# V of batch 1 through SyncE's hardware queue: a blockwise causal attention with a maxout MLP on one core

## The chip, the core and the metric

One core of one Trainium2 chip runs the whole program. The metric is the device time of one execution in microseconds, the median of several executions; smaller is better.

## What is computed

```python
B, H, S, D = 8, 8, 576, 64                       # attention: 8 batches, 8 heads
scores = q @ k.T / sqrt(D)                       # causal by blocks of 64: block_i >= block_j
attn   = softmax(scores)
x      = (attn @ v).transpose(0, 2, 1, 3).reshape(B * S, H * D)      # 4608 x 512
out    = maximum(x @ w1, x @ w2) @ w_out         # 512 -> 1024 -> 512, float32
```

The inputs q, k, v and the weights are float32 in HBM; the matmuls run in bf16.

## The kernel before

**Tiling.** Heads are worked in pairs: pair p is two heads of batch p // 4, and a group g is two pairs, so group g holds pairs 2g and 2g+1. There are 32 pairs, 16 groups and 8 batches. For each group, q and k come as fp32 (`load_qk`, one DMA each on SyncE's queue, L120), are cast to bf16 (`cast`, L132, nearly always on GpSimd), transposed by TensorE (L352) and copied out of PSUM (L360) to `qT` and `kT`. Scores (L371, L389) go through ACT's exp (L395) to `aT`, GpSimd zeroes the masked corners (`mask`, L400), and `av` (L479) multiplies by V. DVE divides by the row sums (L485, L486) and writes `xp`. `x_out` brings `xp` transposed into `xT`: TensorE transposes (L517, L519), and two copies (L522, L523), on DVE unless other engines are given. From group 4 on, DMA transposes do it instead (L497).

**xT** is one tile of 128 partitions, 4 rows (`NDM`) of 4672 bf16 columns each; a row holds 128 of the 512 model features, and columns are tokens. `x_out` of group g = 2b + u writes rows 2u and 2u+1 in one copy, at the tokens of batch b. Late tokens of `xT` are not needed early, so parts of them hold other data at first: `w2_sb`, the four blocks of w2, lies in row 1 (three blocks of 1024 columns from token 1536 on) and row 3 (one block).

**The MLP.** max(a, b) = b + max(a - b, 0), so the kernel forms d = w1 - w2 (`diff_w`, DVE, L162), h = x d, g = max(h, 0) (L220, DVE), and out = x M + g w_out with M = w2 w_out (`bT_unit` L227 and L229, `m_unit` L238 and L243). These matmuls are cut into units that generators yield one by one; `fill(n)` places the next ones between the steps of attention, and units become ready when the tokens they need are in `xT`.

**Order.** The schedule is manual: each engine runs its instructions in the order in which the program issues them. The framework adds the semaphore waits, from which parts of which tiles an instruction reads and writes. `load_qk(..., gated=True)` first issues a one-column memset on GpSimd into the tile to be loaded, so that the DMA on SyncE can start only when GpSimd has got to that point.

**V.** `load_v(b, c)` loads rows c of batch b by GpSimd's software queue (L136), which casts to bf16 on the way, into `vv_r[b % 3]`, a buffer of 5 chunks x 8 heads x 65 columns (the 65th holds ones, for the row sums). Chunks 0 to 3 have 128 rows, chunk 4 has 64. For batch 1 the five loads are issued in the opening part, between the loads of group 3 and an `x_out`:

```python
    load_qk(3, (SP, SP), gated=True)    # L651
    for c in range(NCH):
        load_v(1, c)                    # L653
    x_out(0, 2, NCH)                    # L654: rows 0, 1 of xT, tokens 256 to 575
    diff_w(1)
    fill(2)
```

A little later come `x_out(1, 2, NCH)` (L663: rows 2 and 3, the same tokens), the casts of group 3, and `pool_work(4)`, which issues the gates and loads of group 4 (L544). Batch 1 is first used by `av` of pair 4.

Of the kernel before, what the change touches and what calls it, by code (L numbers as in the profile page):

```python
# [8 lines left out]
FP32 = mybir.dt.float32  # L9
# [5 lines left out]
def kernel(  # L15
# [10 lines left out]
    nc = tc.nc  # L26

    B, H, S, D = q.shape
    P = 128
    BLK = 64  # L30
# [23 lines left out]
    NCH = 5  # L54
# [39 lines left out]
    NV, NA, NT = 3, 4, 4  # L94
# [3 lines left out]
    vv_r = [ring.tile([P, NCH, H, D + 1], BF16, name=f"vv{r}") for r in range(NV)]  # L98
    aT_r = [ring.tile([P, 2, AW + APAD], BF16, name=f"aT{r}") for r in range(NA)]
    xT = ring.tile([P, NDM, NTOK + BLK], BF16, name="xT")  # L100
# [9 lines left out]
    dve, pool, act = nc.vector.tensor_copy, nc.gpsimd.tensor_copy, nc.scalar.copy  # L110

    def load_qk(g, queues, gated=False):
        b, u = divmod(g, GPB)
        for nm, src, queue in (("q", q, queues[0]), ("k", k, queues[1])):
            if queue is None:
                continue
            raws[nm, g] = t = raw.tile([P, 2, RPP * D], FP32, name=f"{nm}raw")
            if gated:
                nc.gpsimd.memset(t[:, 0, :1], 0.0)
            queue.dma_start(  # L120
                out=t[:],
                in_=src[b, 4 * u:4 * u + 4].rearrange(
                    "(s h) (p t) d -> (h p) s (t d)", h=2, t=RPP),
            )

    def cast(nm, g, parts):
        t = raws[nm, g].rearrange("p s (t d) -> p t s d", d=D)
        if (nm, g) not in qk_n:
            qk_n[nm, g] = qkn.tile([P, RPP, 2, D], BF16, name=f"{nm}n")
        n = qk_n[nm, g]  # L130
        for copy, j0, j1 in parts:
            copy(out=n[:, j0:j1], in_=t[:, j0:j1])  # L132

    def load_v(b, c):
        rows = min(P, S - c * P)
        nc.gpsimd.dma_start(  # L136
            out=vv_r[b % NV][P - rows:, c, :, :D],
            in_=v[b, :, c * P:c * P + rows, :].rearrange("h p d -> p h d"),
        )

    w1r = moe_w1.rearrange("(c p) f -> p c f", p=P)
    w2r = moe_w2.rearrange("(c p) f -> p c f", p=P)
# [4 lines left out]
    for j in range(d_ff // WB):  # L147
        row, n = (1, j) if j < 3 else (3, 0)
        t0 = 3 * S - 3 * BLK + n * NDM * WB
# [21 lines left out]
    dve, pool, act = nc.vector.tensor_copy, nc.gpsimd.tensor_copy, nc.scalar.copy  # L171
# [19 lines left out]
    for c in range(2):  # L191
        load_v(0, c)
# [310 lines left out]
    def x_out(g, t0=0, t1=NCH, copies=(dve, dve)):  # L503
        b, u = divmod(g, GPB)
        if x_by_dma(g):
            if u == GPB - 1:
                done_tokens[0] = (b + 1) * S
            return
        xp = xps[g]
        n = t1 - t0  # L510
        n_odd = min(t1, NCH - 1) - t0
        pe = ps_m.tile([P, 2, n, BLK], BF16, name="ps_xe", tag="m")
        po = ps_m.tile([P, 2, n_odd, BLK], BF16, name="ps_xo", tag="m")
        for s in range(2):
            for t in range(t0, t1):
                src = xp[:, s, t].rearrange("p a d -> p (a d)")
                nc.tensor.transpose(pe[:, s, t - t0, :], src[:BLK], ident[:BLK, :BLK])  # L517
                if t < NCH - 1:
                    nc.tensor.transpose(po[:, s, t - t0, :], src[BLK:], ident[BLK:, BLK:])  # L519
        dst = xT[:, 2 * u:2 * u + 2, b * S + t0 * P:b * S + t1 * P].rearrange(  # L520
            "p s (t h w) -> p s t h w", h=2, w=BLK)
        copies[0](out=dst[:, :, :, 0], in_=pe[:])  # L522
        copies[1](out=dst[:, :, :n_odd, 1], in_=po[:])  # L523
        if u == GPB - 1:
            done_tokens[0] = min(b * S + t1 * P, (b + 1) * S)
# [8 lines left out]
    def fill_of(g):  # L534
        if g == NG - 1:
            return 45
        left = 5 - g if g < 5 else 2 - (g - 5) % 2
        return -(-max(0, ready() - KEEP) // left)


    def pool_work(s):
        g, i = divmod(s, 2)
        if s == 4:
            load_qk(4, (SP, SP), gated=True)  # L544
        elif s == 5:
            load_qk(5, (SP, SP), gated=True)
            cast("q", 4, ((pool, 0, RPP),))
            cast("k", 4, ((pool, 0, RPP),))
        else:
            if i == 1 and g + 3 < NG:  # L550
                load_qk(g + 3, (SP, SP), gated=True)
            if i == 1 and g + 2 < NG:
                cast("q", g + 2, ((pool, 0, RPP),))
                cast("k", g + 2, ((pool, 0, RPP),))
            nb, j = divmod(s + 2, HP)
            if nb < B:
                for c in ((0, 1), (2, 3), (4,), ())[j]:
                    load_v(nb, c)
# [33 lines left out]
    for c in range(2, NCH):  # L592
        load_v(0, c)
# [56 lines left out]
    pad_keys(5)  # L650
    load_qk(3, (SP, SP), gated=True)  # L651
    for c in range(NCH):
        load_v(1, c)  # L653
    x_out(0, 2, NCH)  # L654
    diff_w(1)
    fill(2)
# [14 lines left out]
    n = fill_of(GPB)  # L671
    fill(n // 2)
    transposes("q", 3, (dve, act))()
    pool_work(4)
    fill(n // 3)
    transposes("k", 3, (dve, act))()
    pad_keys(6)
    pad_keys(7)
    pool_work(5)
    fill(n - n // 2 - n // 3)  # L680

    for g in range(GPB + 1, NG):
        a, b = 2 * g, 2 * g + 1
        old = done_tokens[0]
        if x_due:
            x_out(x_due.pop())
        n, new = fill_of(g), done_tokens[0]
        region(tile_0(a), tile_1(a))
        lo, hi = max(3, n // 18), n * 2 // 9
        for p, tiles in ((a, lambda: (tile_2(a), tile_0(b))), (b, lambda: (tile_1(b), tile_2(b)))):  # L690
            if p == a and x_by_dma(g - 2):
                done_tokens[0] = old
            rest = fill(hi)
            done_tokens[0] = new
            fill(rest)
            av_with(p - LAG, lo)
            if p % 2 and x_by_dma(g - 1):
                x_dma(g - 1)
            copy_out = t_pair(p)
            outs = tiles()  # L700
            copy_out()
            region(*outs)
            if p % 2 and g + 1 < NG:
                pad_keys(p + 1)
                pad_keys(p + 2)
            pool_work(p)
        x_due.append(g - 1)
        fill(n - 2 * (lo + hi))
# [49 lines left out]
```

The softmax here doesn't subtract the row's maximum and nothing guards it: scores larger than these inputs give would overflow.

## Time and profile before

| | |
|---|---|
| median of 3 runs | 258.6 us (258.4 to 258.81) |
| the profiled execution: its own time | 260.0 us |
| span of the profiled execution, first to last instruction | 258.2 us |
| granted TensorE clock over the span | 1.00 |
| PE busy | 247.4 us (96%) |
| DVE / ACT / POOL busy | 136.1 / 143.2 / 110.4 us |
| HBM read / written | 34.60 / 9.44 MB |
| V loads on GpSimd's queue | 40 (32 of 128 KB, 8 of 64 KB by their bf16 size), 33.7 us of issue on POOL |

How to read it: times in the views are microseconds from the start of the span, unless marked ns. PE is TensorE's matmuls, PEld its weight loads, DVE VectorE, ACT ScalarE, POOL GpSimd, SP SyncE; an engine with a q behind it is its sequencer. A line such as L522 is a line of the kernel before. In a timeline a row gives start, length, engine, line, operation, tiles (out<-in), shape, count, and in brackets the idle time before it with what ended it. In the chain of waits a row gives start, length, and what the end of the program was waiting for then. In a table by stretches, each engine's busy time stands with its number of instructions, followed by the granted clock, the mean share of the 16 DMA engines (over 1 where packets of one engine overlap) and GB/s.

### The profile page before, as it was taken

How to read it: one execution, taken by the hardware profiler on the slowest of the kernel's cores; microseconds unless marked ns; L12 is line 12 of the kernel's file. 1: busy time of each engine (PE TensorE's matmuls, PEld its weight loads, DVE VectorE, ACT ScalarE, POOL GpSimd, SP SyncE). 2: the span in 40 equal slices, each digit the busy share in tenths (PEclk: the TensorE clock that was granted, in tenths of full speed). 3: DMA queues.
4: the chain of work that ended last, by engine and by line, in shares of the span. 5: the costliest groups of instructions: out<-in, count | busy, mean ns of one | idle time of the engine just before them, and what ended most of it. 6: DMA issues, size and time to landing. Idle time of an engine off the chain costs nothing.

```text
span 258.2 us, 7195 instructions
## 1 busy us (share of the span) xinstructions
PE 247.4 (96%) x2983; PEld 139.1 (54%) x2983; DVE 136.1 (53%) x299; ACT 143.2 (55%) x200; POOL 110.4 (43%) x274
## 2 busy tenths in 40 slices
PE   7598899799999999999999999999999999999995
PEld 2346678646555555555555554546464655444444
DVE  4967986556584428451845184518550853443200
ACT  2798854476574857586757665766576431000111
POOL 1987950584637263726382638163813010000000
PEclk9999999999999999999999999999999999999999
DMA  6999999499569995998599949985977122202122
GB/s 244 316 206 307 217 251 246 156 102 253 129 162 257 144 188 135 245 154 225 114 244 143 186 145 224 168 196 141 91 109 110 44 56 80 83 0 81 43 104 99
DMA packets 71265, 41.30 MB, mean 160 GB/s; under 512 B 53568, under 2 KB 58048, under 8 KB 71232
## 3 DMA queue, kind: packets, MB, share of 16 engines
q1 hardware_dynamic: 28544, 31.27, 43.4%
q0 software_dynamic: 42272, 8.92, 39.9%
q10 hardware_dynamic: 416, 0.66, 0.7%
q8 instruction: 23, 0.38, 0.6%
q14 instruction: 10, 0.08, 0.1%
HBM read 34.60 MB, written 9.44 MB: 171 GB/s over the span
## 4 chain that ended last, share of the span: by engine, by line
PE 84%; DMA 8%; POOL 3%; ACT 2%; issue 1%; DVE 0%; SPq 0%; POOLq 0%; ACTq 0%
PE ps_y L257 36%; PE ps_h L215 22%; PE ps_o L479 10%; PE ps_s L371 8%; DMA qraw<-in_q_dram 5%; DMA kraw<-in_k_dram 3%; PE ps_qT L352 2%; PE ps_kT L352 2%; PE ps_w L341 1%; ACT aT L395 1%; PE ps_y L272 1%; PE ps_M L238 1%; POOL kn L132 1%; PE ps_s L389 1%; ACT qT L360 1%
## 5 line engine op out<-in xcount | busy, mean ns | idle before, releaser
L395 ACT ACTIVATE aT<-ps_s 128x1024 bf16<-128x1024 f32 (+2 forms) x100 | 95.8, 996 | 25.8 <-PE ps_s L371 24.2
L257 PE MATMUL ps_y<-wo_sb,g 128*128 128x512 bf16 x280 | 69.8, 379 | 0.0
L215 PE MATMUL ps_h<-xT,d_sb 128*128 128x512 bf16 (+3 forms) x320 | 69.2, 358 | 0.3 <-DVE d_sb L162 0.3
L220 DVE TENSOR_SCALAR g<-ps_h 128x512 bf16<-128x512 f32 (+3 forms) x80 | 50.7, 636 | 30.6 <-PE ps_h L215 28.8
L400 POOL MEMSET aT<- 64x128 bf16 x124 | 22.4, 200 | 81.8 <-ACT aT L395 81.2
L485 DVE RECIPROCAL rec<-ps_o 128x4 f32<-128x4 f32 (+1 forms) x64 | 12.1, 188 | 62.5 <-PE ps_o L479 61.7
L215 PEld LDWEIGHTS <-d_sb 128*128 128x128 bf16 x320 | 29.0, 98 | 29.1 <-issue 2.7
L479 PEld LDWEIGHTS <-aT 128*128 128x128 bf16 x960 | 37.2, 98 | 13.5 <-issue 0.8
L262 ACT COPY y<-ps_y 128x512 f32<-128x512 f32 x31 | 18.2, 587 | 44.5 <-PE ps_y L257 36.1
L257 PEld LDWEIGHTS <-g 128*128 128x128 bf16 x280 | 25.8, 98 | 29.8 <-issue 2.0
L479 PE MATMUL ps_o<-vv,aT 128*128 128x65 bf16 x960 | 39.8, 194 | 0.0
L257 PE MATMUL ps_y<-m_sb,xT 128*128 128x512 bf16 x140 | 38.2, 380 | 0.0
L136 POOL DMA_DIRECT2D vv<-in_v_dram x40 | 33.7, 848 | 1.6 <-issue 1.2
L371 PE MATMUL ps_s<-qT,kT 64*128 64x64 bf16 (+6 forms) x344 | 31.2, 280 | 1.6 <-ACT kT L360 0.7
L486 DVE TENSOR_TENSOR xp<-ps_o,rec 128x256 bf16<-128x256 f32 (+1 forms) x64 | 31.4, 491 | 2.2
L360 ACT COPY qT<-ps_qT 128x576 bf16<-128x576 bf16 (+1 forms) x17 | 10.3, 614 | 19.9 <-PE ps_qT L352 19.9
L132 POOL CAST qn<-qraw 128x1152 bf16<-128x1152 f32 (+1 forms) x16 | 16.9, 1058 | 9.1 <-DMA qraw<-in_q_dram 9.1
L257 PEld LDWEIGHTS <-xT 128*128 128x128 bf16 x140 | 12.2, 98 | 15.1 <-issue 3.5
L371 PEld LDWEIGHTS <-kT 64*128 64x128 bf16 x344 | 12.3, 94 | 11.0 <-issue 6.2
L132 POOL CAST kn<-kraw 128x1152 bf16<-128x1152 f32 (+1 forms) x15 | 17.1, 1140 | 1.4 <-DMA kraw<-in_k_dram 1.4
L360 ACT COPY kT<-ps_kT 128x576 bf16<-128x576 bf16 x15 | 9.6, 639 | 14.4 <-PE ps_kT L352 14.4
L207 POOL COPY g<-g 128x512 bf16<-128x512 bf16 x8 | 4.9, 614 | 20.7 <-DVE g L220 20.3
(58 smaller groups left out, 161.8 us busy)
## 6 DMA issues: line engine op xcount, KB each, us to landing
qraw<-in_q_dram SPq DMA_DIRECT2D x16, 576.0 KB, 5.0
out_dram<-y SPq DMA_DIRECT2D x35, 256.0 KB, 3.7
kraw<-in_k_dram SPq DMA_DIRECT2D x15, 576.0 KB, 5.8
vv<-in_v_dram POOLq DMA_DIRECT2D x32, 128.0 KB, 5.7
w1raw<-in_moe_w_dram POOLq DMA_DIRECT2D x4, 512.0 KB, 8.1
xT<-in_moe_w_dram POOLq DMA_DIRECT2D x4, 256.0 KB, 8.6
wo_sb<-in_moe_w_out_dram POOLq DMA_DIRECT2D x2, 512.0 KB, 10.0
kraw<-in_k_dram ACTq DMA_DIRECT2D x1, 576.0 KB, 5.6
```

The costliest lines, as they stand in the source:

```text
L132: copy(out=n[:, j0:j1], in_=t[:, j0:j1])
L136: nc.gpsimd.dma_start(out=vv_r[b % NV][P - rows:, c, :, :D], in_=v[b, :, c * P:c * P + rows, :].rearrange("h p d -> p h d"),)
L215: nc.tensor.matmul(pt[:, :w], d_sb[:, c, f * P:(f + 1) * P], xT[:, c, t0:t0 + w], start=(c == 0), stop=(c == NDM - 1),)
L220: nc.vector.tensor_scalar_max(g[:, f, m:m + w], pt[:, :w], 0.0)
L257: nc.tensor.matmul(py[:], lhs, rhs, start=(n == 0), stop=(n == len(terms) - 1),)
L262: (dve if i < 2 else act)(out=y[:], in_=py[:])
L360: (copy or copies[i])(out=t[:, p0 * RPP:p1 * RPP].rearrange("q (p j) -> q p j", j=RPP), in_=pts[i][:, :, p0:p1].rearrange("q j p -> q p j"),)
L371: nc.tensor.matmul(ps[:, hh, col:col + w], kT[r, k0:k0 + P], qT[r, q0:q0 + w], start=True, stop=True,)
L395: nc.scalar.activation(out=aT_r[p % NA][:, :, a0:a0 + w], in_=ps[:, :, :w], func=AF.Exp, scale=scale,)
L400: (eng or nc.gpsimd).memset(aT_r[p % NA][BLK:, :, a0:a0 + BLK], 0.0)
L479: nc.tensor.matmul(po[:, gi, hh, :], a[:, hh, a0:a0 + P], vv[:, c, h0 + 2 * hh, :], start=(mm == 0), stop=(mm == n_mm - 1),)
L486: nc.vector.tensor_mul(xp[:, :, ts[0]:ts[0] + n, p % 2].rearrange("q s t d -> q t s d"), po[:, :, :, :D], rec[:, :n].to_broadcast([P, n, 2 ...
```

## The change

V of batch 1 no longer goes by GpSimd's queue. `stage_v` puts it, still fp32, by SyncE's hardware queue into parts of `xT` that no token needs yet: chunks 0 to 2 in row 0 (three slots of 1024 bf16 columns from token 1536 on), chunks 3 and 4 in row 2 (two slots). The five transfers stand where the five `load_v` stood, so on SyncE's queue they come after q and k of group 3 and before those of group 4. In `pool_work(4)`, behind the gates of group 4, GpSimd casts the five chunks into `vv_r[1]`. All other batches are as before.

```diff
+    def v_stage(c):
+        row, n = (0, c) if c < 3 else (2, c - 3)
+        t0 = 3 * S - 3 * BLK + n * 2 * H * D
+        return xT[:, row, t0:t0 + 2 * H * D].bitcast(FP32).rearrange("p (h d) -> p h d", h=H)
+
+    def stage_v(b, c):
+        rows = min(P, S - c * P)
+        nc.sync.dma_start(
+            out=v_stage(c)[P - rows:],
+            in_=v[b, :, c * P:c * P + rows, :].rearrange("h p d -> p h d"),
+        )
+
+    def cast_v(b, c, copy):
+        rows = min(P, S - c * P)
+        copy(out=vv_r[b % NV][P - rows:, c, :, :D], in_=v_stage(c)[P - rows:])
...
         if s == 4:
             load_qk(4, (SP, SP), gated=True)
+            for c in range(NCH):
+                cast_v(1, c, pool)
...
     load_qk(3, (SP, SP), gated=True)
     for c in range(NCH):
-        load_v(1, c)
+        stage_v(1, c)
     x_out(0, 2, NCH)
```

## The prediction

> **What bounds the kernel now.** I first read the busy times: PE is busy for 247.4 of 258.2 us, so idle PE time is 10.8 us in all, and only that can be won. Then the chain of waits, from 24 to 48 us, the part that the change touches:
>
> ```profile
> 26.58 1.14 POOL kz L378 x2
> ...
> 28.34 8.94 DMA kraw<-in_k_dram
> 37.27 0.05 issue
> 37.33 1.15 POOL kn L132
> ...
> 38.55 7.51 DMA qraw<-in_q_dram
> ...
> 46.18 1.16 POOL qn L132
> 47.34 0.05 issue
> 47.38 0.44 PE ps_qT L352 x18
> ```
>
> The chain runs over k of group 3, its cast, the gate, q of group 4 and its cast; PE then waits for that cast. From 48 us on the chain is PE alone. PE's timeline shows the two places that matter:
>
> ```profile
> 27.51 1.04 PE L215 MATMUL ps_h<-xT,d_sb 128*128 128x256 bf16 x8
> ...
> 47.38 0.44 PE L352 MATMUL ps_qT<-ident,qn 64*128 64x64 bf16 x18 [1.61 <-POOL qn L132]
> ```
>
> The second row has the only large gap after 28 us, 1.61 us: all that faster loads here can win. Before the first row stands DVE, which from 25 to 34 us works with hardly a break:
>
> ```profile
> 24.98 0.75 DVE L360 COPY kT<-ps_kT 128x576 bf16<-128x576 bf16 x1
> 25.64 0.35 DVE L522 COPY xT<-ps_xe 128x384 bf16<-128x384 bf16 x1
> 25.91 0.28 DVE L523 COPY xT<-ps_xo 128x256 bf16<-128x256 bf16 x1
> 26.11 1.22 DVE L162 TENSOR_TENSOR d_sb<-w1raw,xT 128x1024 bf16<-128x1024 f32 x1
> ```
>
> The copies at 25.64 are `x_out(0, 2, NCH)`, issued just behind the V loads. PE's h at 27.51 needs the `d_sb` that ends at 27.33. Last, the table by stretches, for the DMAs (last columns: clock, DMA share, GB/s):
>
> ```profile
> 27.30:31.40 4.10, 3.75 (x64) 3.13 (x61) 4.07 (x10) 3.69 (x6) 4.10 (x9) 1.00 1.44 195
> 31.40:36.40 5.00, 4.59 (x51) 3.31 (x48) 4.20 (x9) 4.03 (x5) 2.99 (x10) 1.00 1.26 302
> 36.40:39.50 3.10, 3.10 (x40) 2.23 (x39) 2.82 (x6) 0.64 (x1) 1.23 (x3) 1.00 2.34 157
> 39.50:42.50 3.00, 3.00 (x45) 2.23 (x43) 2.05 (x5) 0.64 (x1) 0.60 (x4) 1.00 2.01 173
> ```
>
> By the packet records, q and k of group 3, issued at 27.8 and 28.3, get their first packet at 31.5: until then the weight loads on GpSimd's queue hold the engines, and they end at 37.3. The last q, k packets go at 36.0 on most engines, 36.85 on the slowest; k lands at 37.28. V of batch 1 runs mainly from 35 to 41.5.
>
> **What the Trainium skill says.** "DMA: Bandwidth & Descriptors", section "Queues, rings and completion order": each DMA engine takes descriptors of one ring in order and alternates between rings. The trace agrees as far as it goes (SP's load of group 3 shares the engines with the weights from 31.5 on); so V on SP's ring comes after q and k of group 3. Section "SWDGE vs HWDGE vs iDMA": only GpSimd's queue casts in flight, which is why fp32 is staged and five casts are added; no run here shows it. Section "Why small descriptors are slow": a 256-byte packet takes 11 cycles of a DMA engine, 3 of them overhead. The trace's 256-byte packets on SP's queue (DMA transposes) take 18 ns, against 93 ns for 2304 bytes, so they are dearer per byte. "TensorE: Matmul & The Clock Gate", Part 1: an idle window of about 3.4 us halves the clock, and a busy one restores it. The trace shows the recovery: the first warm-up matmuls start every 0.43 us, and from 4.1 us on every 0.22.
>
> **The change part by part.**
>
> *Removed from POOL*: five DMA issues, 27.73 to 31.92, 4.19 us. They lie beside POOL's wait for exps (the masks that follow come when ACT lets them), so they bring nothing by themselves.
>
> *Added to POOL*: five casts of 128x512. The cast of 128x1152 takes 1.06 to 1.14 us, so a cast takes some 0.5 us by size and five 2.6 us. They stand between the gate of group 4 and `pad_keys`, where POOL waits 3.13 us for kT (41.69 in the trace of before), and hide there if V has landed by then: 0. With the cover gone they would delay `pad_keys`, the gates of group 5 and the cast of q of group 4, which PE takes at 47.38, by up to 2.6 us.
>
> *Added to SP*: five DMAs of 1024 (the last 512) packets of 256 bytes, behind q, k of group 3, ahead of those of group 4. The issue of q takes 0.37 us and of a transpose, with 640 packets, about 1.3; even at 2 us each the first three are out by 35, before the engines have finished k. SP has nothing else before 38.5. Group 4 then follows V in the ring.
>
> *A new wait on DVE, which the diff doesn't show.* In the compiled order with its waits, the xT copy of `x_out(0, 2, NCH)`, which waited only for PE, now waits also for the landings of V chunks 0, 1 and 2; that of `x_out(1, 2, NCH)` waits for chunks 3 and 4. The data don't overlap: tokens 256 to 575 are written, V lies from 1536 on. But the copy covers two rows, and taken as one run of addresses from row 0, token 256 to row 1, token 575 it holds all of row 0 behind token 256: chunks 0 to 2. Rows 2 and 3 likewise hold chunks 3 and 4. The w2 blocks in rows 1 and 3 are in neither run, and there before has no such wait. So the framework must be taking runs, not elements.
>
> *Its cost.* DVE reaches the copy at 25.64, when V isn't even issued. V's packets start when k of group 3 is through: 36.0 to 36.85, less a little as V no longer competes on the other ring; I take 36.4. Chunks 0 to 2 are 3072 packets, 192 for each of 16 engines. The price of such a packet from HBM isn't in the trace. From below: on GpSimd's queue V's packets (256 bytes read, 128 written) pass at 1205 in one us, or 13.3 ns per engine: 2.55 us. From above: twice the 18 ns of the transposes' packets, 6.9 us. I take 18 ns, 3.46 us. The end adds 0.4 (k: last packet 36.85, landing 37.28). Landing: 36.4 + 3.5 + 0.4 = 40.3 (39.3 to 43.7). DVE is late by 40.3 - 25.64 = **14.7 us** (13.7 to 18.1).
>
> *Who waits.* Behind the copy on DVE stand `d_sb`, the copies of bT, the divisions, g. PE does bT, two tiles of scores and one `av`, and stops at the h of 27.51, whose PSUM buffer and `d_sb` both want DVE. ACT and the masks run dry, POOL stops at the masks of pairs 4 and 5, and the gate of group 4 waits there. The end moves by the whole 14.7. The second copy (30.33 before, 4.7 after the first) finds chunks 3 and 4 landed, as they need 96 more packets, 1.7 us: 0.
>
> *Given back*: q, k of group 3 and V wait in SBUF when work resumes; the casts follow the masks at once, the gate of group 4 comes about 1.6 us earlier against PE's work (masks to 34.55, two casts of 1.15, so 36.9 where it was 38.5), and its loads find idle DMA engines (5.0 us is the median landing). The gap of 1.61 us goes: -1.6 (bounds -1.6 and 0).
>
> *Clock*: after 15 us of idleness PE starts slow. Over some 3 us it would lose 1.5, of which the DVE-bound stretch absorbs part: +1.0 (0.3 to 1.5).
>
> *Sum*: +14.7 - 1.6 + 1.0 = +14.1 us. On the profiled execution that is a span of 258.2 + 14.1 = 272.3 and a time of 260.0 + 14.1 = 274.1; the median of before lies 1.4 below its profiled execution, and so 258.6 + 14.1 = **272.7 us**.
>
> **Rivals.**
> 1. *V's packets cost twice* (36 ns): the landing at 43.7, +18.1 - 1.6 + 1.5 = +18: 276.6. For it: small packets are dear per byte. Against it: 18 ns on the same queue. 0.12.
> 2. *V lands early*: the hardware ring gets its turn sooner with V in it. V can't be issued before 28.8; with the 3.5 us of the fastest V landing in the trace, and three chunks, hardly before 33: +7.4 - 1.6 + 1.0 = +6.8: 265.4. Against it: q of group 3 got nothing before 31.5. 0.08.
> 3. *It does what it seems to*: the wait costs nothing, V stays off the second ring, q of group 4 lands before PE wants it, and the 1.61 us go: 257.0. For it: the 173 GB/s of 39.5 to 42.5, where both rings compete. It decides if chunks 0 to 2 land before DVE arrives at 25.64, which the gate at 27.7 excludes, or if that wait isn't there. 0.02.
> 4. *Nothing*: what is won and a short wait cancel: 258.6. 0.01.
>
> **How the numbers follow.** The likeliest case has 0.77 and gives 272.7; its own bounds are 271.0 (13.3 ns: 13.7 - 1.6 + 0.3 = +12.4) and 274.4 (27 ns, half-way to rival 1: 5.2 us of packets, +16.4 - 1.6 + 1.0 = +15.8). The range takes in rival 1 with a margin, and at the lower end goes beyond 271.0 towards rival 2, since k of group 3 may finish sooner with no V on the other ring: 268.5 to 277.5. A measurement of this kernel tells apart about 0.2%, 0.5 us. Faster by more: 0.02; within: 0.01; slower: 0.97, all cases but the last two.
>
> **What would show it.** In the profile of the changed kernel: a gap of about 15 us on DVE ahead of the xT copy, ended by a DMA into xT; one on PE ahead of h (before: 27.51), then slow matmuls for some 3 us; no gap ahead of qT of group 4; the chain through V's DMA; POOL casts of 0.5 us with no wait. An xT copy still at 25.6, or V landing before 33, would make it wrong.

## The result and the profile after

| | before | after |
|---|---|---|
| median of 4 runs | 258.58 us | 275.5 us |
| lowest to highest | 258.4 to 258.81 | 274.59 to 277.28 |
| profiled execution: time, span | 260.0, 258.2 us | 275.6, 273.8 us |
| mean granted TensorE clock | 1.00 | 0.969 |

The ratio is 1.0662 (95% interval 1.0608 to 1.0716): the changed kernel is 16.9 us slower. The prediction was slower by 14.1, at 272.7, in a range of 268.5 to 277.5.

In the changed kernel's file the lines from `load_w` to `pool_work` stand 16 higher (the xT copy is L538, h L231, av L495, qT and kT L368). Its chain of waits (start, length, what) now runs through the staging of V:

```profile
29.00 0.64 SPq L148
...
29.68 11.08 DMA xT<-in_v_dram
...
40.88 0.09 DVE xT L538
...
41.16 0.28 DVE xT L539
41.44 1.14 DVE d_sb L178
...
42.63 1.89 PE ps_h L231 x8
```

The entry at 29.68 is the third V chunk, from its issue on SP to its landing at 40.76. DVE's timeline shows who waited for it (in brackets the idle time before the row, and what ended it):

```profile
24.95 0.75 DVE L376 COPY kT<-ps_kT 128x576 bf16<-128x576 bf16 x1
40.88 0.36 DVE L538 COPY xT<-ps_xe 128x384 bf16<-128x384 bf16 x1 [15.18 <-DMA xT<-in_v_dram]
41.16 0.28 DVE L539 COPY xT<-ps_xo 128x256 bf16<-128x256 bf16 x1
41.35 1.22 DVE L178 TENSOR_TENSOR d_sb<-w1raw,xT 128x1024 bf16<-128x1024 f32 x1
```

Before, the same copy started at 25.64 with no gap: it is 15.24 us late. On PE's timeline the gap stands ahead of h, as the prediction placed it, and there is none ahead of qT of group 4 (62.80):

```profile
26.73 0.92 PE L495 MATMUL ps_o<-vv,aT 128*128 128x65 bf16 x24
42.63 1.89 PE L231 MATMUL ps_h<-xT,d_sb 128*128 128x256 bf16 x8 [14.98 <-DVE d_sb L178]
...
57.49 0.44 PE L368 MATMUL ps_kT<-ident,kn 64*128 64x64 bf16 x18
...
62.80 0.43 PE L368 MATMUL ps_qT<-ident,qn 64*128 64x64 bf16 x18
```

The eight h matmuls take 1.89 us, where they took 1.04. The table by stretches tells why: the column behind POOL's is the granted clock, and it is 0.50 for the first 5.8 us after the gap:

```profile
27.30:42.50 15.20, 0.34 (x12) 0.22 (x8) 1.62 (x4) 1.34 (x2) 0.40 (x2) 0.64 1.11 225
42.50:48.30 5.80, 5.67 (x44) 3.95 (x45) 5.24 (x11) 2.85 (x4) 0.34 (x2) 0.50 0.00 0
48.30:60.00 11.70, 11.58 (x139) 8.42 (x137) 8.41 (x17) 5.19 (x8) 7.04 (x18) 0.99 0.31 103
```

On GpSimd the five casts run without a wait, 0.62 us each where 0.5 was predicted, and q of group 4 is cast well before PE takes it:

```profile
54.11 2.97 POOL L155 CAST vv<-xT 128x512 bf16<-128x512 f32 x5
...
59.40 1.14 POOL L132 CAST qn<-qraw 128x1152 bf16<-128x1152 f32 x1
```

### The profile page after: what moved, and what is told of

Its sections match the earlier page's. It is cut to its first block, busy times and chain, and to the rows that moved or that the text cites. A ratio compares the mean times of both kernels' runs of the same rounds, so it can differ in the third digit from the quotient of the medians.

```text
span 273.8 us, 7176 instructions
## 1 busy us (share of the span) xinstructions
PE 246.6 (90%) x2949; PEld 140.6 (51%) x2983; DVE 136.4 (50%) x299; ACT 143.3 (52%) x200; POOL 108.2 (40%) x274
## 4 chain that ended last, share of the span: by engine, by line
PE 84%; DMA 6%; ACT 4%; issue 2%; DVE 2%; SPq 0%; ACTq 0%; DVEq 0%
PE ps_y L273 33%; PE ps_h L231 23%; PE ps_o L495 10%; PE ps_s L387 8%; DMA xT<-in_v_dram 4%; ACT aT L411 3%; PE ps_M L254 3%; PE ps_qT L368 2%; DMA qraw<-in_q_dram 2%; PE ps_kT L368 2%; PE ps_y L288 1%; DVE qn L132 1%; PE ps_w L357 1%; PE ps_bT L243 1%; PE ps_s L405 1%
## 5 line engine op out<-in xcount | busy, mean ns | idle before, releaser
L231 PE MATMUL ps_h<-xT,d_sb 128*128 128x512 bf16 (+3 forms) x306 | 69.2, 364 | 16.5 <-DVE d_sb L178 15.0
L273 PE MATMUL ps_y<-wo_sb,g 128*128 128x512 bf16 x275 | 69.1, 379 | 0.4 <-issue 0.3
L231 PEld LDWEIGHTS <-d_sb 128*128 128x128 bf16 x320 | 29.7, 100 | 44.9 <-DVE d_sb L178 15.1
L495 PEld LDWEIGHTS <-aT 128*128 128x128 bf16 x960 | 37.2, 98 | 13.5 <-issue 0.8
L495 PE MATMUL ps_o<-vv,aT 128*128 128x65 bf16 x960 | 39.8, 194 | 0.0
L273 PE MATMUL ps_y<-m_sb,xT 128*128 128x512 bf16 x128 | 36.5, 380 | 1.2 <-issue 0.8
L387 PE MATMUL ps_s<-qT,kT 64*128 64x64 bf16 (+6 forms) x344 | 31.5, 283 | 1.9 <-ACT kT L376 0.7
L136 POOL DMA_DIRECT2D vv<-in_v_dram x35 | 29.4, 845 | 1.6 <-issue 1.2
L132 POOL CAST qn<-qraw 128x1152 bf16<-128x1152 f32 (+1 forms) x16 | 16.9, 1057 | 4.6 <-DMA qraw<-in_q_dram 4.6
L376 DVE COPY kT<-ps_kT 128x576 bf16<-128x576 bf16 (+2 forms) x19 | 12.9, 686 | 0.5 <-PE ps_kT L368 0.5
```

Source lines behind the costliest of these rows:

```text
L136: nc.gpsimd.dma_start(out=vv_r[b % NV][P - rows:, c, :, :D], in_=v[b, :, c * P:c * P + rows, :].rearrange("h p d -> p h d"),)
L231: nc.tensor.matmul(pt[:, :w], d_sb[:, c, f * P:(f + 1) * P], xT[:, c, t0:t0 + w], start=(c == 0), stop=(c == NDM - 1),)
L273: nc.tensor.matmul(py[:], lhs, rhs, start=(n == 0), stop=(n == len(terms) - 1),)
L376: (copy or copies[i])(out=t[:, p0 * RPP:p1 * RPP].rearrange("q (p j) -> q p j", j=RPP), in_=pts[i][:, :, p0:p1].rearrange("q j p -> q p j"),)
L387: nc.tensor.matmul(ps[:, hh, col:col + w], kT[r, k0:k0 + P], qT[r, q0:q0 + w], start=True, stop=True,)
L495: nc.tensor.matmul(po[:, gi, hh, :], a[:, hh, a0:a0 + P], vv[:, c, h0 + 2 * hh, :], start=(mm == 0), stop=(mm == n_mm - 1),)
```

## The experiments

The theory: the xT copy waits for V's landings because the framework takes a copy over two rows of xT as one run of addresses; that wait is nearly the whole loss, and the half clock after it the rest. The main rival: the staging itself is dear (fp32, 256-byte packets, issues on SP, casts). All comparisons are with the kernel before run beside them on the same chip; its median there was 258.99, 258.74 and 259.06 us in the three groups e1 to e4, e5 to e8, e9 and e10. The changed kernel was not run again beside them: its 275.5 us belong to the 258.58 of the table above.

### Is it the wait? e1, e2 and e10

**e1** moves only the place of the staging.

```diff
-    for c in range(NCH):
-        stage_v(1, c)
     x_out(0, 2, NCH)
+    for c in range(3):
+        stage_v(1, c)
...
     x_out(1, 2, NCH)
+    for c in range(3, NCH):
+        stage_v(1, c)
```

> The changed kernel with only the place of the staging altered: chunks 0 to 2 are issued behind x_out(0, 2, NCH), chunks 3 and 4 behind x_out(1, 2, NCH). Same queue, same slots, same casts. Theory (the wait of the xT copy for the landings is the whole loss): DVE's gap of 15.2 us is gone, the xT copy stands near 25.6 again; q and k of group 3 have SP's ring for themselves until V follows, q of group 4 lands near 44 instead of 46, so that PE's gap of 1.61 us ahead of qT of group 4 goes too: 257.0 us, between 256.6 and 258.6. Rival (fp32 V with 256-byte packets and its back-pressure on SP is itself dear): SP is held until 39.5 by V's issues, q of group 4 lands after 47, av of pair 4 waits for the casts: 260 us or more.

259.54 us, ratio to before 1.0017 (1.0002 to 1.0031): above what the theory gave, below the rival's 260. DVE's timeline has the copy back in its place, with no gap:

```profile
25.38 0.75 DVE L376 COPY kT<-ps_kT 128x576 bf16<-128x576 bf16 x1
26.04 0.35 DVE L538 COPY xT<-ps_xe 128x384 bf16<-128x384 bf16 x1
```

**e2** leaves the staging where it is and splits the copies by row.

```diff
+        if g < 2 and t0:
+            for s in range(2):
+                copies[0](out=dst[:, s, :, 0], in_=pe[:, s])
+                copies[1](out=dst[:, s, :n_odd, 1], in_=po[:, s])
+        else:
             copies[0](out=dst[:, :, :, 0], in_=pe[:])
             copies[1](out=dst[:, :, :n_odd, 1], in_=po[:])
```

> The changed kernel with the staging where it is, but the xT copies of x_out for groups 0 and 1 (second part) split into one copy for each row of xT. Theory (the framework takes a copy over two rows as one run of addresses): a copy of one row holds no staged chunk, the wait is gone although V is issued ahead of it; the four extra copies, about 0.2 us each, lie in the stretch where DVE bounds PE: 257.0 + 0.5 = 257.5 us, between 257 and 259. Rival (the wait comes from the order of the program, any writer of xT behind the staging waits): 275.5 us as the changed kernel.

259.50 us, ratio 1.0017 (0.9998 to 1.0036), again a little above what was expected. Its DVE timeline (L540 and L541 are the copies of one row):

```profile
24.99 0.75 DVE L376 COPY kT<-ps_kT 128x576 bf16<-128x576 bf16 x1
25.66 0.25 DVE L540 COPY xT<-ps_xe 128x192 bf16<-128x192 bf16 x1
25.82 0.21 DVE L541 COPY xT<-ps_xo 128x128 bf16<-128x128 bf16 x1
```

The same elements of the same tile are written behind the same staging, and the wait is gone: what decides is not the order of the program but the span of one access. The four copies end at 26.3 where two ended at 26.2, so the split costs about 0.1 us, not 0.5.

**e10** adds the wait to the kernel before: V goes by GpSimd's queue as it did, and chunks 0 to 2 are also staged, where nothing reads them (`stage_v` as in the change).

```diff
     for c in range(NCH):
         load_v(1, c)
+    for c in range(3):
+        stage_v(1, c)
     x_out(0, 2, NCH)
```

> The kernel before, V of batch 1 by GpSimd's queue as it was, and in addition chunks 0 to 2 staged in xT by SP ahead of x_out(0, 2, NCH), where nothing reads them. Only the wait of the xT copy and its transfers are added; no cast, no chunk left out on GpSimd. Theory (the wait for those landings is the loss): the two streams of V share the engines from 36 us on, so the landing is 1 to 4 us later than the 40.8 us of the changed kernel: 276 to 280 us. Rival (the loss needs what else changed: casts on GpSimd, V missing from its queue): under 262 us.

280.03 us, ratio 1.0810 (1.0782 to 1.0838), at the upper end of what was expected, with the copy 4.9 us later than in the changed kernel:

```profile
45.79 0.36 DVE L538 COPY xT<-ps_xe 128x384 bf16<-128x384 bf16 x1 [19.80 <-DMA xT<-in_v_dram]
```

So the wait, with the transfers that it waits for, makes the loss without the rest of the change, and without the wait the rest of the change costs about 0.5 us. That e1 and e2 did not reach the 257.0 and 257.5 that were expected is taken up with e5.

### How long the wait is: e3

Only chunk 0 is staged ahead of the copy; 1 and 2 follow it, 3 and 4 stand as in e1.

```diff
-    for c in range(NCH):
-        stage_v(1, c)
+    stage_v(1, 0)
     x_out(0, 2, NCH)
+    for c in (1, 2):
+        stage_v(1, c)
```

> The changed kernel with only chunk 0 issued ahead of x_out(0, 2, NCH); chunks 1 to 4 behind the x_outs as in e1. Theory (DVE waits for the last landing in the run of addresses that it writes): chunk 0 was issued at 28.36 and took 10.3 us, so DVE resumes near 38.7 instead of 40.9 and the end comes some 2.1 us sooner than in the changed kernel: 273.4 us. Rival (what costs is q and k of group 3 in the ring ahead of V, whatever the number of chunks, or the cold clock alone): the same to within 0.5 us as the changed kernel, 275 to 276.

273.21 us, ratio 1.0579 (1.0538 to 1.0620); DVE's row:

```profile
39.20 0.36 DVE L538 COPY xT<-ps_xe 128x384 bf16<-128x384 bf16 x1 [13.26 <-DMA xT<-in_v_dram]
```

The gap is 1.92 us shorter for two chunks less. In the changed kernel chunk 1 landed at 39.7 and chunk 2 at 40.76: about 1.05 us for each chunk of 1024 packets. So of 15 us two come from the number of chunks. The rest is that V is issued 2.7 us after DVE is ready for the copy (28.36 and 25.70) and then stands behind q and k of group 3, the last of which lands at 36.8; that order itself was not varied.

### The clock: e4

The changed kernel with matmuls of zeros in PE's gap, into a PSUM buffer that nobody reads:

```diff
     av(3, [2, 3, 4])
+    pw = ps_s.tile([P, 2, 512], FP32, name="ps_keep", tag="s")
+    for _ in range(64):
+        nc.tensor.matmul(pw[:, 0], zeros[:, :P], zeros[:], start=True, stop=True)
```

> The changed kernel with 64 matmuls of zeros into a free PSUM buffer behind av of pair 3, which keep PE busy for some 13.8 us of its 15 us gap; nothing reads them. Theory (the half clock after the gap costs the 1.85 us by which PE's work is later at kT of group 3 than DVE was at its copy): no stretch at half clock, 275.5 - 1.9 = 273.6 us, and a spread from run to run as small as before (0.2 us instead of 2.7). Rival (DVE bounds that stretch, and the clock costs next to nothing): 275.0 to 276 us.

273.99 us, ratio 1.0586 (1.0558 to 1.0613), 1.5 below the changed kernel. The granted clock is 1.00 throughout, and PE's timeline has the eight h matmuls at 1.05 us again:

```profile
28.35 13.97 PE L679 MATMUL ps_keep<-zeros 128*128 128x512 bf16 x62
43.16 1.05 PE L231 MATMUL ps_h<-xT,d_sb 128*128 128x256 bf16 x8 [0.84 <-DVE d_sb L178]
```

The wait is still there: the xT copy starts at 41.42, after a gap of 15.15 us. From that copy to PE's kT of group 3 pass 14.63 us here (to 56.05) and 16.61 in the changed kernel (40.88 to 57.49). Before it was 14.76, from 25.64 to this row:

```profile
40.40 0.44 PE L352 MATMUL ps_kT<-ident,kn 64*128 64x64 bf16 x18
```

The half clock costs 2.0 us by the traces and 1.5 by the medians. The four runs went from 273.59 to 274.18, those of the changed kernel from 274.59 to 277.28; that the half clock makes that spread is not shown, since the executions of 275.6 and 277.28 have the same mean clock, 0.969.

### What the median of before contains: e5, e6, e7

The kernel before twice more and e1 once more, one profiled execution each, no edit.

> The kernel before, unchanged, for a second profile. Theory (the 1.4 us by which the profiled execution of before lay above its median are the 1.61 us gap ahead of qT of group 4, which other executions don't have or have shorter): an execution near 258.5 us shows a gap ahead of qT of group 4 of at most 0.5 us, with the loads of group 4 landing before 45. Rival (the gap is in every execution and the 1.4 us lie elsewhere, in the opening or at the end): a gap of 1.3 to 1.9 us whatever the time.

> The kernel before, unchanged, for a third profile. As for e5: by the theory the time moves with the gap ahead of qT of group 4, about one for one; by the rival the gap stays at 1.3 to 1.9 us and the time doesn't follow it.

> The kernel of e1 unchanged, for a second profile. Its median was 259.54 us where its profiled execution ran 259.37 with a gap of 0.16 us ahead of qT of group 4. Theory (its casts of V wait for the landings, and GpSimd's later steps stand behind them, so that the gap varies too): an execution at 259.5 or more shows a gap of 0.5 us or more there. Rival (the time is lost elsewhere): a gap of at most 0.3 us at any time.

The rows of qT of group 4 on PE's timeline, of e5 (260.26 us), e6 (259.2 us) and e7 (260.4 us) in this order:

```profile
47.65 0.44 PE L352 MATMUL ps_qT<-ident,qn 64*128 64x64 bf16 x18 [1.78 <-POOL qn L132]
```

```profile
46.58 0.44 PE L352 MATMUL ps_qT<-ident,qn 64*128 64x64 bf16 x18 [0.36 <-POOL qn L132]
```

```profile
47.35 0.44 PE L368 MATMUL ps_qT<-ident,qn 64*128 64x64 bf16 x18 [1.41 <-POOL qn L132]
```

The gap comes and goes. e6 has 1.42 us less of it than e5, an opening that ran 0.35 us later, and is 1.06 us faster: the difference to within 0.01. The first profile fits as well. PE's bT matmuls behind the opening start at 25.68 there, 25.78 in e5 and 26.13 in e6; less its gap, and less what its opening ran later than the first, each of the three executions takes 258.4 us. In this kernel it is the landing of q of group 4 that moves: 7.5 us after its issue in the first profile, 7.7 in e5, 6.4 in e6. Neither new execution was at before's median, so the case of no gap wasn't seen; that the median of 258.6 holds little of it is inferred from the 258.4.

In e1 the gap is there too at times: 0.16 us in the execution of 259.37, 1.41 in that of 260.4. In e7 GpSimd's timeline shows what stands ahead of the cast that PE waits for:

```profile
42.64 0.62 POOL L155 CAST vv<-xT 128x512 bf16<-128x512 f32 x1 [1.61 <-DMA xT<-in_v_dram]
44.25 1.29 POOL L155 CAST vv<-xT 128x512 bf16<-128x512 f32 x2 [1.00 <-DVE m_sb L259]
...
46.16 1.14 POOL L132 CAST qn<-qraw 128x1152 bf16<-128x1152 f32 x1
```

The cast of q itself has no wait; it comes behind V's casts, which wait for the staged chunks. (The view names DVE's m_sb ahead of the fourth; that chunk's landing at 44.1 falls beside it, and which of the two came last isn't settled.) The load of q is late too, as SP's timeline shows:

```profile
29.31 12.22 SPq L148 DMA_DIRECT2D xT<-in_v_dram  x5
41.63 0.56 SPq L120 DMA_DIRECT2D qraw<-in_q_dram  x1
```

The five issues of V hold SP until 41.5, so q of group 4 is issued at 41.63 where it was 38.55. It lands 4.4 us later, 0.1 us ahead of its cast; in e2, with a gap of 1.04 us, the cast does wait for it, 0.24 us. Less gap and opening, e1 and e7 still take 258.8 and 258.9 us: some 0.4 to 0.5 us of their loss lies elsewhere and was not found.

### Two tries to beat both: e8, e9

**e8**: the kernel before with the gates and loads of group 4 ahead of the casts of group 3.

```diff
         if s == 4:
-            load_qk(4, (SP, SP), gated=True)
+            pass
...
+    load_qk(4, (SP, SP), gated=True)
     cast("q", 3, ((pool, 0, RPP),))
     cast("k", 3, ((pool, 0, RPP),))
```

> The kernel before, with V of batch 1 by GpSimd's queue as it was, and only the gates and loads of group 4 moved ahead of the casts of group 3 on GpSimd, so that SP issues them near 34.6 instead of 38.5. If the gap ahead of qT of group 4 is what executions of before lose, and the loads of group 4 end it, the gap is gone in every execution: 258.0 us, 0.5 to 1.0 below before's median on the same chip, with a smaller spread. Rival (the engines are full with V and the weights until 42, so an earlier issue brings no earlier landing, or delays k of group 3): the same as before to within 0.3 us, or slower by up to 1 us.

259.5 us, ratio 1.0024 (1.0008 to 1.0040). The gap ahead of qT is gone, and stands ahead of av of pair 4, for V:

```profile
47.06 0.80 PE L479 MATMUL ps_o<-vv,aT 128*128 128x65 bf16 x15 [1.35 <-DMA vv<-in_v_dram]
```

**e9**: staged V behind q of group 4, whose gate moves ahead, and cast behind it.

```diff
-            load_qk(4, (SP, SP), gated=True)
+            load_qk(4, (None, SP), gated=True)
+            cast("q", 4, ((pool, 0, RPP),))
             for c in range(NCH):
                 cast_v(1, c, pool)
...
+    load_qk(4, (SP, None), gated=True)
+    for c in range(NCH):
+        stage_v(1, c)
     cast("q", 3, ((pool, 0, RPP),))
```

(This is set against the changed kernel. The staging ahead of x_out and the later cast of q of group 4 are taken out.)

> A version that tries to beat both kernels: V of batch 1 staged as fp32 by SP behind both x_outs and behind q of group 4, whose gate moves ahead of the casts of group 3 on GpSimd; then k of group 4. GpSimd casts q of group 4 first and then V. If the engines' order of work, not their amount, makes the gap near 46 us, q of group 4 lands near 38.5, V's last chunk near 43.5, and only av of pair 4 may wait 0.5 us for a cast: 258.2 us, 0.3 to 0.8 below before on the same chip. Rival (the transfers up to 46 us are a fixed amount that fills the engines, and what is moved ahead pushes the rest back): V lands at 44.5 or later, the gap stands ahead of av of pair 4 instead, 258.7 to 260 us.

259.77 us, ratio 1.0026 (1.0014 to 1.0038). Again the wait has moved to av of pair 4, now for V's casts:

```profile
45.56 0.43 PE L495 MATMUL ps_o<-vv,aT 128*128 128x65 bf16 x9 [0.33 <-POOL vv L155]
46.24 0.34 PE L495 MATMUL ps_o<-vv,aT 128*128 128x65 bf16 x6 [0.24 <-POOL vv L155]
```

Both rivals held: what was moved ahead pushed the rest back. No version tried beats the kernel before.

## Why the prediction was right, and where its sum was short

*The mechanism* was right in each place: the copy on DVE, the PE gap ahead of h, the chain through V's DMA, the casts at no cost. e1, e2 and e10 show it from both sides. That the run of addresses is what counts, which the prediction could only infer, e2 supports, and the trace of the changed kernel adds to it: ahead of the first xT copy DVE waits for the semaphores of chunks 0, 1 and 2 and not of 3 and 4, although these stand ahead of it in the program too, so it isn't the whole tile either.

*The number* was less good than the range makes it look. 275.5 us lies above the likeliest case's own bounds, 271.0 to 274.4, and only 1.1 us below the 276.6 of the first rival; the range held it because it took that rival in. What tells them apart is the landing, below.

*The wait*: predicted 14.7 us, measured 15.24. The landing came at 40.76, predicted 40.3. Two terms missed in opposite directions: by the packet records V's first packet went at 35.3, not 36.4, while k was still running, and from there to the landing it took 5.5 us where 3.9 were taken; the weight loads ran beside it until 37.9. The price of a packet was right: 18 ns in the packet records, 1.05 us a chunk. It had been taken over from transposes, with bounds of 13.3 and 36 ns, and that it fits so well is in part luck.

*The issues on SP*: "even at 2 us each the first three are out by 35" failed. The third took 7.60 us, from 29.68 to 37.28, and ended just after k of group 3 had landed at 36.8; that a full ring held it is inferred from this. In the changed kernel this costs nothing, as SP's next load is issued at 54.17; in e1 and e7 it delays q of group 4.

*The clock*: predicted +1.0, bounded by 1.5. PE's kT of group 3 moved from 40.40 to 57.49, 17.09 us, which is 1.85 more than DVE's copy. The price of half speed was right, its length not: the prediction took 3 us from the opening, the trace shows 5.9 (42.63 to 48.55 in its clock records), half of it lost less what DVE's pace covered. The Trainium skill, "TensorE: Matmul & The Clock Gate", Part 1, gives a window of about 3.4 us. The half clock lasted 17.07 us here, 13.65 in e3 and 20.48 in e10, five, four and six times 3.41, so the traces agree on the window. That work starting inside one window has to wait for the end of the next would explain the 5.9 us here and 4.4 in e3 from PE's first matmul to the full clock; the 3.1 in e10 fit only if a window that is nearly filled counts. This wasn't tested further.

*Given back*: predicted -1.6; from kT of group 3 to qT of group 4 the delay falls from 17.09 to 15.42, -1.67. Right for this execution. The step that failed is the translation to the median: "the median of before lies 1.4 below its profiled execution, and so 258.6 + 14.1". By e5 and e6 the 1.4 us were for the most part that same gap, so the median had little of it to give back, and it was subtracted twice. The changed kernel's profiled execution (275.6) and its median (275.5) agree. Against the profiled execution the forecast was 274.1 for 275.6. At the median 0.5 (wait), 0.85 (clock) and 1.4 (gap) make up the miss of 2.8 us to within 0.1. The expectations of e1 and e2, 257.0 and 257.5, fell in the main by the same mistake.

*The rivals*: packets at double price and an early landing are excluded by the packet records and the landing at 40.76 (43.7 and 33 by those rivals); "it does what it seems to" by the wait. e1 shows what was left of that last one with the wait removed: nothing gained, 0.17% lost.

## What to carry to other kernels

Data put into a free part of a tile that is still being written can tie the two together even where no element overlaps: look at the compiled order with its waits for each writer of that tile, and either put the new writer behind the old ones in the program or cut the old access so that its run of addresses doesn't enclose the guest. Before a gap in a profile is counted as winnable, profile the kernel a second time: a gap that comes and goes is in the profile's time but perhaps not in the median. Where several loads are due at one point and the engines are full, a change of their order moves the wait to the one put last.

## What the runs showed of the hardware

Of three 1024-packet transfers in a row on SP's queue, behind q and k of group 3, the first two were issued in 0.59 and 0.64 us, and the third held SP for 7.60 us. And SP's ring got nothing while the weight loads of GpSimd's queue were dense: in the kernel before, q of group 3 was issued at 27.8 and had its first packet at 31.5, in the changed kernel at 27.1 and 30.9. The prediction's remark that the trace agrees with engines that alternate between rings holds only from then on; why they didn't before was not tried.
